# The second layer's quarters 3 and 4: their second product by seven products of halves, and the order of all steps read from a table

## The chip, the cores and the metric

The kernel runs on one core of a Trainium2 chip. The metric is the time of one execution on the device, in microseconds (us). All inputs and outputs are 4-byte floats in the chip's main memory, and the weights arrive as 8-byte words that the kernel itself turns back into 4-byte floats. The engines are named as the profile names them: PE (matmul), PEld (its weight loads, shown apart), DVE (vector), ACT (scalar), POOL, and SP, whose queue issues most of the DMA transfers.

## The reference

A linear attention over 4 x 8 heads of 576 tokens gives 2304 tokens of 512 values each. Two layers of the same shape follow, 512 to 2048 to 512, with a softplus between the two products of the first and an ELU between those of the second:

```python
kv = np.einsum('bhsd,bhse->bhde', k, v)
out = np.einsum('bhsd,bhde->bhse', q, kv)
x = out / np.sqrt(np.mean(out * out, axis=-1, keepdims=True) + 1e-06) * g_norm
h = x @ w_in                       # layer 1: 2304x512 @ 512x2048
g = np.maximum(h, 0.0) + np.log1p(np.exp(-np.abs(h)))
x = g @ w_out                      # 2304x2048 @ 2048x512
h = x @ w_in2                      # layer 2, the same shapes
g = np.where(h > 0.0, h, np.exp(np.minimum(h, 0.0)) - 1.0)
return g @ w_out2
```

## The kernel before

**Precision.** PE works here on 4-byte values that it rounds, so each operand is split into a high and a low part, and a product is three matmuls: high by high, low by high, high by low.

**Tiling.** The 2304 tokens are six blocks of T = 384, taken in three pairs (p). The 2048 inner values are 16 chunks of 128, taken in four quarters (q) of four chunks, each quarter as two pairs of chunks (f). One *slot* is one pair of blocks by one pair of chunks. There are 48 slots: layer 1 has slots 0 to 23, layer 2 slots 24 to 47, with six slots to a quarter, so that layer 2's quarters 3 and 4 are slots 36 to 47. Two slots that follow each other (f = 0, 1) are a *group*; groups 18 to 23 are those two quarters.

**First product.** From slot 4 on it is a seven-product scheme (Strassen's in Winograd's form): the 2 x 2 halves of tokens and of the weights are combined so that seven products of halves, numbered 1 to 7, take the place of eight. `product` (line 788) issues one of them as six matmuls of 384 columns into the PSUM banks A, B or C of the slot. `slot_h` (line 886) ties them together: after product 1, ACT copies A to C (line 928), and product 6 waits for that copy; after products 6 and 7 ACT or DVE copies A to the tiles hj and hk (lines 903, 905), for which products 7 and 4 wait; DVE adds B to hk after product 5 and to hj after product 3 (line 913). Bank B has one buffer: product 5 of the next slot waits for the add to hj, the slot's *closing add*.

**Between.** `elu` (line 996) makes layer 2's activation with ACT and DVE, in a temporary of three buffers (`"e"`). `slot_parts` (line 1222) splits the result for both blocks into G.

**Second product.** In layer 1's quarters 2 to 4 it is by sevens too: `slot_sevens` (line 1050) makes the sums of the halves, and `out_sevens` and `out_piece` (lines 1114, 1121) issue the products in *pieces*. Everywhere else, all of layer 2 included, `slot_out` and `slot_piece` (lines 1234, 1249) multiply plainly: for each block, chunk and third of the tokens three matmuls of 512 columns, 72 to a group; in the last block the last third is cut into two of 256 columns. `block_sum` (line 640) adds the bank to the sums in SBUF, or in the last quarter to an output tile that goes out. `by_sevens` (line 239) says where the sevens are used.

**Weights.** `conv` (line 289) turns a raw chunk into floats (two ACT and three DVE instructions), `split` (line 337) into high and low part, and `split_pair` with `split_sums` (lines 385, 414) makes the sums of halves for the sevens. There is room for about one quarter of weights.

**Order.** All of this is written as strands that run side by side. `Order.run` (line 131) is a planner: it holds costs of each step and keys of urgency, and writes down next whichever step it reckons can start first. PE's steps come from `main` (line 1422), where `STEPS` and `SEVENS` (lines 1309, 1322) say how many pieces stand between the products. The instructions of each engine run in the order in which they were written.

## Time and profile before

| | us |
|---|---|
| median of 3 runs | 804.38 |
| lowest, highest | 804.06, 806.32 |
| the profiled execution | 803.55 |
| its span, first to last instruction | 801.4 |
| PE busy | 788.1 |
| DVE busy | 609.5 |
| ACT busy | 499.2 |
| mean granted clock of PE | 0.998 |

The profiled execution lies 0.83 us under the median, and 2.15 us of it lie outside the span. A matmul's "us" in the timeline includes its way through the array and overlaps its successor; what one costs in a full stream is the distance from its start to the next one's start. The same holds for DVE and ACT, where an instruction's duration is longer than the distance to the next by 0.08 to 0.11 us.

### The profile page before, as it was taken

The numbers are of one execution on the slowest core, as the hardware profiler recorded it, in microseconds if no ns is written. First come the engines' busy times: TensorE is split into PE (matmuls) and PEld (weight loads), VectorE is DVE, ScalarE is ACT, GpSimd is POOL, SyncE is SP. The second block draws the span as 40 slices with busy tenths as digits, with TensorE's granted clock in tenths as the row PEclk, the third lists the DMA queues.
The fourth block names the chain that finished last, engine by engine and source line by source line (L and its number), as shares of the span: only waits on it lengthen the run. The fifth ranks groups of instructions, "written<-read, shape, count | busy, mean of one in ns | idle before, by whom it ended". The sixth has DMA issues, their size and how long they took to land.

```text
span 801.4 us, 12301 instructions
## 1 busy us (share of the span) xinstructions
PE 788.1 (98%) x4586; PEld 744.2 (93%) x4586; DVE 609.5 (76%) x1056; ACT 499.2 (62%) x939; POOL 58.5 (7%) x62
## 2 busy tenths in 40 slices
PE   8999999999999999999997999999999999999998
PEld 7899999999999999999997988988988988989987
DVE  3888887788988889897999976756776768675344
ACT  3886767675675575685677876764754645555331
POOL 3534400000000000000000000000000000000000
PEclk9999999999999999999999999999999999999999
DMA  9999768859668868968284767667567566475512
GB/s 302 335 341 325 274 261 273 295 190 301 234 211 285 263 223 280 294 208 272 77 301 171 270 234 278 245 240 251 185 248 249 170 246 254 151 254 216 182 65 92
DMA packets 46235, 191.25 MB, mean 239 GB/s; under 512 B 5216, under 2 KB 6496, under 8 KB 46176
## 3 DMA queue, kind: packets, MB, share of 16 engines
q1 hardware_dynamic: 44016, 184.57, 64.6%
q0 software_dynamic: 2160, 5.90, 3.9%
q8 instruction: 36, 0.59, 0.3%
q14 instruction: 23, 0.19, 0.1%
HBM read 146.80 MB, written 37.75 MB: 230 GB/s over the span
## 4 chain that ended last, share of the span: by engine, by line
PE 83%; DMA 6%; DVE 5%; ACT 2%; issue 1%; POOL 1%; SPq 0%; DVEq 0%; ACTq 0%
PE A L816 21%; PE B L816 10%; PE acc L1269 10%; PE acc L1270 10%; PE acc L1268 10%; PE A L1152 7%; PE C L816 5%; DMA raw<-w 4%; PE A L844 3%; PE B L1152 3%; PE C L1152 2%; PE po L560 1%; DMA acc_sb<-kv_rest 1%; DMA acc_sb<-kv 1%; PE kv L493 1%
## 5 line engine op out<-in xcount | busy, mean ns | idle before, releaser
L1270 PE MATMUL acc<-wlo,G 128*128 128x512 f32 (+1 forms) x292 | 113.4, 388 | 0.0
L1269 PE MATMUL acc<-whi,G 128*128 128x512 f32 (+1 forms) x292 | 113.3, 388 | 0.0
L1268 PE MATMUL acc<-whi,G 128*128 128x512 f32 (+1 forms) x292 | 112.7, 386 | 0.0
L816 PE MATMUL A<-x,wx 128*128 128x384 f32 x528 | 107.4, 337 | 5.3 <-ACT C L928 3.6
L816 PEld LDWEIGHTS A<-x,wx 128*128 128x128 f32 x528 | 93.3, 189 | 6.8 <-ACT C L928 4.3
L816 PE MATMUL A<-x,whi 128*128 128x384 f32 x352 | 98.6, 335 | 0.6 <-ACT hk L903 0.6
L317 ACT ACTIVATE c<-raw 128x512 f32<-128x512 f32 x64 | 42.9, 671 | 51.7 <-DMA raw<-w 46.1
L816 PEld LDWEIGHTS A<-x,whi 128*128 128x128 f32 x352 | 64.7, 188 | 1.7 <-ACT hk L903 0.9
L1270 PEld LDWEIGHTS acc<-wlo,G 128*128 128x128 f32 x292 | 54.8, 188 | 11.2
L1268 PEld LDWEIGHTS acc<-whi,G 128*128 128x128 f32 x292 | 54.9, 188 | 9.9
L1269 PEld LDWEIGHTS acc<-whi,G 128*128 128x128 f32 x292 | 54.8, 188 | 9.8
L816 PE MATMUL A<-x,wlo 128*128 128x384 f32 x176 | 59.1, 336 | 0.0
L913 DVE TENSOR_TENSOR hj<-hj,B 128x384 f32<-128x384 f32 x44 | 24.3, 552 | 42.9 <-PE B L816 42.7
L347 ACT CAST whi<-q 128x512 fp32r<-128x512 f32 x64 | 39.6, 618 | 24.4 <-PE acc L1269 11.1
L351 DVE TENSOR_TENSOR wlo<-q,whi 128x512 fp32r<-128x512 f32 x64 | 44.0, 687 | 12.9 <-ACT whi L347 12.7
L816 PE MATMUL B<-x,wx 128*128 128x384 f32 x264 | 52.8, 334 | 0.0
L816 PE MATMUL B<-x,whi 128*128 128x384 f32 x176 | 52.1, 336 | 0.0
L816 PE MATMUL C<-x,whi 128*128 128x384 f32 x176 | 52.1, 336 | 0.0
L928 ACT COPY C<-A 128x384 f32<-128x384 f32 x42 | 19.6, 466 | 47.9 <-PE A L816 44.5
L816 PEld LDWEIGHTS B<-x,wx 128*128 128x128 f32 x264 | 46.4, 188 | 0.0
L330 DVE CUSTOM_DVE_ANT_0 q<-c,r 128x1024 uint16<-128x1024 uint16 x64 | 44.0, 687 | 2.1
L325 DVE SCALAR_TENSOR_TENSOR c<-raw,c 128x512 uint32<-128x512 uint32 x64 | 44.0, 688 | 1.0
(231 smaller groups left out, 1901.8 us busy)
## 6 DMA issues: line engine op xcount, KB each, us to landing
x<-spill SPq DMA_DIRECT2D x126, 768.0 KB, 6.2
raw<-w SPq DMA_DIRECT2D x64, 512.0 KB, 5.6
spill<-x SPq DMA_DIRECT2D x42, 768.0 KB, 4.9
acc_sb<-kv SPq DMA_DIRECT2D x16, 512.0 KB, 6.4
acc_sb<-s POOLq DMA_DIRECT2D x15, 384.0 KB, 5.4
out<-o SPq DMA_DIRECT2D x17, 256.0 KB, 2.1
q<-qt SPq DMA_DIRECT2D x9, 256.0 KB, 6.7
q_late<-qt SPq DMA_DIRECT2D x9, 256.0 KB, 6.1
```

What stands on the lines that cost most here:

```text
L317: nc.scalar.activation(c.bitcast(F32), high_f, AF.Copy, scale=2.0**-112)
L325: nc.vector.scalar_tensor_tensor(c, high, 0x80000000, c, op0=ALU.bitwise_and, op1=ALU.bitwise_or)
L330: nc.vector.tensor_tensor(q.bitcast(U32), c, r, op=ALU.add)
L347: nc.scalar.copy(hi, q)
L351: nc.vector.tensor_sub(lo, q, f32(hi))
L816: nc.tensor.matmul(bank[:, :T], w, x, start=start and i == 0, stop=stop and i == len(seq) - 1, skip_group_check=True,)
L844: nc.tensor.matmul(a[:, :T], w, x, start=half == 0 and i == 0, stop=half == 1 and i == len(seq) - 1, skip_group_check=True,)
L913: nc.vector.tensor_add(to, to, bank[:, :T])
L1152: nc.tensor.matmul(a, l, r, start=first and i == 0, stop=last and i == 2, skip_group_check=True)
L1268: nc.tensor.matmul(a, l[0], r[0], start=(u == 0), stop=False)
L1269: nc.tensor.matmul(a, l[1], r[0], start=False, stop=False)
L1270: nc.tensor.matmul(a, l[0], r[1], start=False, stop=(u == QF - 1))
```

## The change

The second product of layer 2's quarters 3 and 4 is computed by seven products of halves, as in layer 1, but with the tokens as rows: the stationary operand is a tile of 128 tokens, the moving one 256 columns of the weights. `by_sevens` returns true there, so the sums of the weights' halves, the sums of the activations' halves and their split follow as in layer 1, behind ELU. `out_piece` issues for each product, slot and part m of the tokens (m = 0 is two tiles of 128, m = 1 the third) six or three matmuls of 256 columns. A new `flush_rows` adds each bank to the SBUF sums with DVE (or, where the result is final, into an output tile, then a DMA of 256 or 128 KB). ELU's temporary is taken from the ring `"s1"`, which has one buffer, in these quarters. The weights' second halves come in as pieces of two chunks.

The planner is gone. `Order.run` reads a table of about 32,000 characters, three to a step (which strand, and which engine or, for PE, whether a product or a piece), so that the order of all engines is fixed there, in both layers. The diff, without the planner's removed lines:

```diff
+    def run(self, table):
+        steps = iter("".join(table.split()))
+        for a, b, letter in zip(steps, steps, steps):
+            s = self.strands[int(a + b, 36)]
+            if s[2] is None:
+                continue
+            self.demand(s[2][1])
             self.now, self.going = s[0], s
             try:
-                s[2] = s[1].send(e)
+                s[2] = s[1].send(self.ENGINES[letter])
             except StopIteration:
-                self.strands.remove(s)
-                continue
-            if e == DMA == s[2][0][0][0]:
-                s[3] = done
+                s[2] = None
...
+TABLE = """
+3pt59p59p59p3pt45t59p59p46t59p59p57t57t47t3qt3pp3pa59p3pa59p3qt3rt59p48p48a59p59p48d3qp59p3rt3st
...
+    SEVENS_FROM = 2
+    OUT_OPS_2 = ((1, 2, 6, 5, 3, 7, 4),) * 3
...
     def by_sevens(layer, q):
-        return layer == 0 and q > 0
+        return q > (0 if layer == 0 else SEVENS_FROM - 1)
...
+        tag = "s1" if a and by_sevens(*slots[s][:2]) else "e"
+        yield ((ACT, act(T if a else 2 * T, True)),), [ring(tag), *ready]
         if not exp_set:
             exp_set.append(s)
             load_set(EXP_SET)
         h = h()[0]
-        e, e_h = sbuf("e", 3, f"e{s}_{b}", (P, 2, T))
+        e, e_h = sbuf(tag, 3 if tag == "e" else 1, f"e{s}_{b}", (P, 2, T))
...
-        bank, a_h = a
-        yield ((ACT, act(T, True)),), [("cc", s)] if b else [("cb", s)]
+        act_of = elu if slots[s][0] else softplus
+        yield from act_of(s, b, h, a, [("cc", s)] if b else [("cb", s)])
         h, h_h = h()
...
+        tiles = range(2 * m, min(2 * m + 2, TT)) if layer else range(1)
+        yield ((PE, 3 * len(tiles) * pe(DM // 2) if layer else 3 * pe(T)),), need
         if f == 0 and o in (1, 5):
             banks[which, m] = psum(("accA", "accT")[o == 5], f"{which}{n}")
-        a = banks[which, m][0][:, :T]
         gh, gl, g_h = g2[s, o]
+        c, n = (0, DM // 2) if layer else (m * P, P)
         if o > 4:
             w = wx_t[layer, fc, 1][0]
-            hi, lo = (w[:, part, o - 5, m * P : m * P + P] for part in range(2))
+            hi, lo = (w[:, part, o - 5, c : c + n] for part in range(2))
         else:
-            c = 256 * (o in (2, 3)) + m * P
-            hi, lo = (w[:, c : c + P] for w in w_t[layer, fc + (o > 2), 1][:2])
+            c += 256 * (o in (2, 3))
+            hi, lo = (w[:, c : c + n] for w in w_t[layer, fc + (o > 2), 1][:2])
         first, last = o in (1, 5) and f == 0, o in (2, 3, 4) and f == FP - 1
-        for i, (l, r) in enumerate(((hi, gh), (lo, gh), (hi, gl))):
-            nc.tensor.matmul(
-                a, l, r, start=first and i == 0, stop=last and i == 2, skip_group_check=True
-            )
+        for k, t in enumerate(tiles):
+            if layer:
+                a = banks[which, m][0][:, k * n : k * n + n]
+                xh, xl = (x[:, t * P : t * P + P] for x in (gh, gl))
+                seq = ((xh, hi), (xh, lo), (xl, hi))
+            else:
+                a = banks[which, m][0][:, :T]
+                seq = ((hi, gh), (lo, gh), (hi, gl))
+            for i, (l, r) in enumerate(seq):
+                nc.tensor.matmul(
+                    a, l, r, start=first and k == i == 0, stop=last and i == 2, skip_group_check=True
...
+        def flush_rows(b, i, name, done, x, x_h):
+
+            rows = acc_sb[2 * p + b].rearrange("p (t n) -> p t n", n=DM)
+            c = slice(DM // 4 * i, DM // 4 * i + DM // 2)
+            to = rows[:, tiles[0] : tiles[-1] + 1, c]
+            x = x.rearrange("p (t n) -> p t n", n=DM // 2)
+            ends = q == NQ - 1 and (o in (2, 3, 4) or o == max(5, 7, key=ops_of(layer, p).index))
+            yield ((DVE, dve(width)),), [ring("q")] if ends else []
+            if ends:
+                r, r_h = sbuf("q", 3, f"o{n_}_{o}")
+                r = r[:, :width].rearrange("p (t n) -> p t n", n=DM // 2)
+                nc.vector.tensor_add(r, to, x)
+            else:
+                nc.vector.tensor_add(to, to, x)
+            if name:
+                mark(name, g, m)
+            if done:
+                drop(x_h)
+            if ends:
+                t0 = (2 * p + b) * T + tiles[0] * P
+                yield ((DMA, dma(P * width * 4)),), []
+                nc.sync.dma_start(
+                    out[t0 : t0 + len(tiles) * P, c].rearrange("(t p) n -> p t n", p=P), r
+                )
+                drop(r_h)
...
+                yield from flush_rows(b, i, name, done, bank[:, :width], bank_h)
+                return
...
-    STEPS = (
-        ((6, '4', 5, 2, '6', '4', 7, 1, 4, '2', 3), (6, '4', 5, 2, '4', 7, '8', 1, 4, 3)),
-        ((6, 2, 5, 7, '5', 1, 4, '1', 3), (6, 2, 5, 7, '1', '16', 4, 1, '1', 3)),
+    PRODUCTS = (
+        ((6, 5, 2, 7, 1, 4, 3), (6, 5, 2, 7, 1, 4, 3)),
+        ((6, 2, 5, 7, 1, 4, 3), (6, 5, 2, 7, 1, 4, 3)),
+        ((6, 2, 5, 7, 1, 4, 3), (6, 2, 5, 7, 4, 1, 3)),
...
+    def main():
+
+        while look("piece") or look(PE):
+            kind = yield ((PE, 0.0),), []
+            step, _, needs = look(kind)
+            order.demand(needs)
+            heads[kind] = None
+            next(step, None)
...
-        order.run()
+        order.run(TABLE)
```

PE's list loses 420 matmuls of 512 columns and 24 of 256, and gains 756 of 256. DVE's list grows from 1056 to 1186 instructions, ACT's from 939 to 984, by the program's own count.

**Place 1, the border of the layers (slots 25 and 26).** ACT's list of before from just behind the copy A25 to hk25 to the copy A26 to C26. G24 and G25 are the split activations of slots 24 and 25, e25 ELU's temporary, c and r steps of `conv`, s11 copies of banks for layer 1's sums, x1 operands of layer 2.

```order
L1227 CAST G24_1_4861<-hk24_4645 128x768
L347 CAST whi1_0_1_4871<-q1_0_1_4802 128x512
L1227 CAST G24_0_4881<-hj24_4559 128x768
L317 ACTIVATE c1_1_1_4884<-raw1_1_1_4852 128x512
L1006 ACTIVATE e25_1_4895<-A25_4667 128x384
L320 ACTIVATE r1_1_1_4898<-raw1_1_1_4852 128x512
L1009 ACTIVATE e25_1_4895<-hk25_4859 128x384
L1180 COPY s11_0_3_4902<-B11_0_4727 128x384
L1011 ACTIVATE e25_1_4895<-e25_1_4895 128x768
L1180 COPY s11_0_3_4902<-B11_1_4738 128x384
L747 CAST x1_0_1_2_4910<-acc_sb2_71 128x768
L928 COPY C26_4913<-A26_4874 128x384
```

The same stretch of ACT's list after the change, with the copy to hk25 itself at its head:

```order
L957 COPY hk25_4859<-A25_4667 128x384
L1321 CAST G24_1_4861<-hk24_4645 128x768
L374 ACTIVATE c1_1_1_4863<-raw1_1_1_4850 128x512
L377 ACTIVATE r1_1_1_4885<-raw1_1_1_4850 128x512
L1274 COPY s128_3_4896<-B11_0_4727 128x384
L1321 CAST G24_0_4898<-hj24_4601 128x768
L1274 COPY s128_3_4896<-B11_1_4734 128x384
L982 COPY C26_4901<-A26_4872 128x384
```

Between the two copies 11 instructions stood; now 6 do. ELU's three steps of slot 25 and two operand casts stand behind the copy to C26.

PE's list there, before: the end of product 3 of slot 25 (bank B25), product 6 of slot 26 (bank A26) and what follows.

```order
L816 MATMUL B25_4835<-x1_0_0_3_4620,wlo1_3_0_4782 128x384
L816 MATMUL B25_4835<-x1_0_0_3_4620,whi1_3_0_4772 128x384 x2
L816 MATMUL A26_4874<-x1_0_1_6_4832,wx1_0_0_4324 128x384 x6
L816 MATMUL C26_4913<-x1_0_1_2_4910,whi1_0_0_4173 128x384
L816 MATMUL C26_4913<-x1_0_1_2_4910,wlo1_0_0_4179 128x384
```

After:

```order
L874 MATMUL B25_4835<-x1_0_0_3_4547,wlo1_3_0_4783 128x384
L874 MATMUL B25_4835<-x1_0_0_3_4547,whi1_3_0_4780 128x384 x2
L1362 MATMUL acc1_0_0_1_0_4916<-whi1_0_1_4852,G24_1_4861 128x512
L1363 MATMUL acc1_0_0_1_0_4916<-whi1_0_1_4852,G24_1_4861 128x512
L1364 MATMUL acc1_0_0_1_0_4916<-wlo1_0_1_4879,G24_1_4861 128x512
L1362 MATMUL acc1_0_0_1_1_4920<-whi1_0_1_4852,G24_1_4861 128x512
L1363 MATMUL acc1_0_0_1_1_4920<-whi1_0_1_4852,G24_1_4861 128x512
L1364 MATMUL acc1_0_0_1_1_4920<-wlo1_0_1_4879,G24_1_4861 128x512
L1362 MATMUL acc1_0_0_1_2_4924<-whi1_0_1_4852,G24_1_4861 128x512
L1363 MATMUL acc1_0_0_1_2_4924<-whi1_0_1_4852,G24_1_4861 128x512
L1364 MATMUL acc1_0_0_1_2_4924<-wlo1_0_1_4879,G24_1_4861 128x512
L874 MATMUL A26_4872<-x1_0_1_6_4831,wx1_0_0_4321 128x384 x6
```

Three pieces (nine matmuls of 512 columns) of slot 24's second product stand between slot 25's product 3 and slot 26's product 6, where there was nothing.

**Place 2, quarter 3 to 4 (slots 41 and 42).** DVE's list of before, from the closing add of slot 41 to the add of B42 to hk42:

```order
L913 TENSOR_TENSOR hj41_7101<-hj41_7101,B41_7109 128x384
L1026 SCALAR_TENSOR_TENSOR hk41_7142<-e41_1_7247,hk41_7142 128x384
L351 TENSOR_TENSOR wlo1_15_0_7285<-q1_15_0_7082,whi1_15_0_7274 128x512
L1229 TENSOR_TENSOR G41_1_7291<-hk41_7142,G41_1_7291 128x768
L1026 SCALAR_TENSOR_TENSOR hj41_7101<-e41_0_7139,hj41_7101 128x384
L905 COPY hk42_7321<-A42_7238 128x384
L1016 SCALAR_TENSOR_TENSOR hj42_7289<-e42_0_7302,C42_7255 128x384
L913 TENSOR_TENSOR hk42_7321<-hk42_7321,B42_7293 128x384
```

After, the first 12 of the 23 rows of the same stretch (acc_sb are the sums in SBUF, A19 and B19 banks of group 19's pieces, xk and xj split sums of halves):

```order
L967 TENSOR_TENSOR hj41_7230<-hj41_7230,B41_7244 128x384
L1125 TENSOR_TENSOR hk40_7127<-hj40_7080,hk40_7127 128x384
L1249 TENSOR_TENSOR acc_sb2_71<-acc_sb2_71,B19_0_7308 128x2x256
L1127 TENSOR_TENSOR hj40_7080<-hk40_7127,hj40_7080 128x384
L1249 TENSOR_TENSOR acc_sb3_72<-acc_sb3_72,A19_0_7152 128x2x256
L1130 TENSOR_TENSOR hj40_7080<-hj40_7080 128x384
L1249 TENSOR_TENSOR acc_sb3_72<-acc_sb3_72,A19_1_7165 128x256
L1071 SCALAR_TENSOR_TENSOR hj41_7230<-e41_0_7368,C41_7186 128x384
L483 TENSOR_TENSOR wx1_14_0_7298<-t2_1_14_0_7300,wx1_14_0_7298 128x256
L1159 TENSOR_TENSOR xk1_40_7428<-hk40_7127,xk0_40_7427 128x768
L1159 TENSOR_TENSOR xj1_40_7431<-hj40_7080,xj0_40_7430 128x768
L1081 SCALAR_TENSOR_TENSOR hj41_7230<-e41_0_7368,hj41_7230 128x384
```

Where 8 instructions stood, 23 stand.

**Place 3, the end (slot 47 and group 23).** DVE's list of before from slot 47's closing add on (o are output tiles):

```order
L913 TENSOR_TENSOR hj47_7920<-hj47_7920,B47_7924 128x384
L1016 SCALAR_TENSOR_TENSOR hk47_7950<-e47_1_8029,A47_7877 128x384
L1026 SCALAR_TENSOR_TENSOR hk47_7950<-e47_1_8029,hk47_7950 128x384
L1026 SCALAR_TENSOR_TENSOR hj47_7920<-e47_0_7934,hj47_7920 128x384
L1229 TENSOR_TENSOR G47_1_8062<-hk47_7950,G47_1_8062 128x768
L1229 TENSOR_TENSOR G47_0_1_8069<-hj47_7920,G47_0_0_8068 128x768
L665 TENSOR_TENSOR o5_0_0_8091<-acc_sb5_74,acc1_3_2_1_0_8041 128x512
L665 TENSOR_TENSOR o5_1_0_8096<-acc_sb5_74,acc1_3_2_1_1_8047 128x512
```

After, a stretch behind the same add (x12, x4, xj, xk are group 23's operands by halves):

```order
L1159 TENSOR_TENSOR xk1_46_8498<-hk46_8260,xk0_46_8497 128x768
L1247 TENSOR_TENSOR o22_0_4_8517<-acc_sb3_72,A22_0_8245 128x512
L1119 TENSOR_TENSOR x12_47_8502<-hj47_8347,x12_47_8502 128x768
L1071 SCALAR_TENSOR_TENSOR hk47_8396<-e47_1_8500,A47_8232 128x384
L1081 SCALAR_TENSOR_TENSOR hk47_8396<-e47_1_8500,hk47_8396 128x384
L1247 TENSOR_TENSOR o22_1_4_8533<-acc_sb3_72,A22_1_8278 128x256
L1141 TENSOR_TENSOR x4_47_8548<-hk47_8396,x4_47_8548 128x384
L1145 TENSOR_TENSOR hk47_8396<-hk47_8396 128x384
L1125 TENSOR_TENSOR hk47_8396<-hj47_8347,hk47_8396 128x384
L1127 TENSOR_TENSOR hj47_8347<-hk47_8396,hj47_8347 128x384
L1130 TENSOR_TENSOR hj47_8347<-hj47_8347 128x384
L1159 TENSOR_TENSOR xj1_46_8487<-hj46_8215,xj0_46_8486 128x768
```

and ACT's list after the change at the same place (C23 are copies of group 23's banks):

```order
L1061 ACTIVATE e47_1_8500<-A47_8232 128x384
L1117 CAST x12_47_8502<-hj47_8347 128x768
L1064 ACTIVATE e47_1_8500<-hk47_8396 128x384
L1066 ACTIVATE e47_1_8500<-e47_1_8500 128x768
L1139 CAST x4_47_8548<-hk47_8396 128x384
L1233 COPY C23_0_8550<-A23_0_8524 128x512
L1233 COPY C23_1_8556<-A23_1_8544 128x256
L1157 CAST xj_47_8587<-hj47_8347 128x768
L1157 CAST xk0_47_8589<-hk47_8396 128x768
```

The operands of the last pieces now take a longer way over both engines, and C23's copies stand behind x4_47.

## Rows read from the trace of the kernel before

**Rows 1.** The page: busy us, share, instructions by engine; the chain by engine.

```profile
PE 788.1 (98%) x4586; PEld 744.2 (93%) x4586; DVE 609.5 (76%) x1056; ACT 499.2 (62%) x939; POOL 58.5 (7%) x62
...
PE 83%; DMA 6%; DVE 5%; ACT 2%; issue 1%; POOL 1%; SPq 0%; DVEq 0%; ACTq 0%
```

**Rows 2.** Waits of PE: engine, line, releaser; us in total, times, longest.

```profile
PE A L816 <- ACT C L928: 3.6, 2, 3.5
...
PE A L816 <- ACT hj L903: 1.4, 1, 1.4
```

**Rows 3.** Timeline of PE near the end: start us, us, what, count.

```profile
782.30 0.39 PE L1268 MATMUL acc<-whi,G 128*128 128x512 f32 x1
...
795.25 0.28 PE L1268 MATMUL acc<-whi,G 128*128 128x256 f32 x1
...
798.00 0.28 PE L1270 MATMUL acc<-wlo,G 128*128 128x256 f32 x1
...
797.52 0.19 PEld L1270 LDWEIGHTS acc<-wlo,G 128*128 128x128 f32 x1
```

**Rows 4.** Timeline of PE at the layers' border.

```profile
429.75 1.20 PE L816 MATMUL A<-x,wx 128*128 128x384 f32 x6
...
434.40 0.51 PE L816 MATMUL B<-x,whi 128*128 128x384 f32 x2
438.40 2.29 PE L816 MATMUL A<-x,wx 128*128 128x384 f32 x6 [3.49 <-ACT C L928]
...
441.70 0.51 PE L816 MATMUL C<-x,whi 128*128 128x384 f32 x2
```

**Rows 5.** Timeline of ACT at the layers' border.

```profile
430.99 0.48 ACT L903 COPY hk<-A 128x384 f32<-128x384 f32 x1
431.36 0.84 ACT L1227 CAST G<-hk 128x768 fp32r<-128x768 f32 x1
432.10 0.62 ACT L347 CAST whi<-q 128x512 fp32r<-128x512 f32 x1
...
433.75 0.67 ACT L317 ACTIVATE c<-raw 128x512 f32<-128x512 f32 x1 [0.29 <-DMA raw<-w]
434.32 0.47 ACT L1006 ACTIVATE e<-A 128x384 f32<-128x384 f32 x1
...
435.66 0.47 ACT L1180 COPY s<-B 128x384 f32<-128x384 f32 x1
436.02 0.85 ACT L1011 ACTIVATE e<-e 128x768 f32<-128x768 f32 x1
...
437.86 0.49 ACT L928 COPY C<-A 128x384 f32<-128x384 f32 x1
```

**Rows 6.** Windows: stretch, its us, then busy us of each engine, granted clock.

```profile
300.00:390.00 90.00, 90.00 (x521) 90.00 (x520) 79.05 (x148) 58.80 (x115) 4.42 (x5) 1.00 0.75 247
392.00:430.00 38.00, 37.56 (x213) 36.35 (x212) 37.15 (x64) 26.08 (x47) 1.75 (x2) 1.00 0.57 194
438.40:441.80 3.40, 3.40 (x11) 3.40 (x12) 2.86 (x4) 2.71 (x5) 0.11 (x1) 0.53 0.91 215
593.00:697.00 104.00, 104.00 (x525) 94.17 (x524) 74.47 (x129) 59.69 (x111) 0.00 (x0) 1.00 0.62 220
697.00:801.00 104.00, 101.28 (x508) 90.55 (x506) 51.69 (x84) 39.88 (x74) 0.00 (x0) 1.00 0.46 162
```

**Rows 7.** Timeline of DVE in the second layer, instructions back to back.

```profile
663.10 0.42 DVE L403 TENSOR_TENSOR t<-q,q 128x256 f32<-128x256 f32 x1
663.43 0.55 DVE L913 TENSOR_TENSOR hk<-hk,B 128x384 f32<-128x384 f32 x1
663.90 0.42 DVE L405 TENSOR_TENSOR t<-q 128x256 f32<-128x256 f32 x1
664.24 0.95 DVE L1229 TENSOR_TENSOR G<-hj,G 128x768 fp32r<-128x768 f32 x1
665.11 0.42 DVE L407 TENSOR_TENSOR t<-q,t 128x256 f32<-128x256 f32 x1
```

More of the change, by code (lines that the diff above doesn't have):

```diff
@@ L168, in run, with demand @@
+        return i < 0 or all(h[0] <= 0 for h in held[: i + 1][-n:])
+    def demand(self, needs):
+        for need in needs:
+            if not self.met(need):
+                raise RuntimeError(f"not there yet: {need}")
+    def run(self, table):
[5 more added lines that the diff above has]
+            self.demand(s[2][1])
             self.now, self.going = s[0], s
@@ L1124, in out_piece @@
         fc = q * QF + 2 * f
[L1125 removed]
+        ends = [max(x, key=ops_of(layer, p).index) for x in ((1, 2), (3, 4), (5, 6, 7))]
         which = {1: "A", 6: "A", 7: "A", 4: "A", 2: "C", 5: "B", 3: "B"}[o]
@@ L1356, in one @@
-    def one(pieces):
-        if pieces:
-            yield pieces.head[1], [pieces.ready]
-            pieces.take()
-    def some_of(pieces, n):
-        for _ in range(n):
-            yield from one(pieces)
-    def filler():
-        for s in range(FP, FILLED):
-            while s in pieces_of and pieces_of[s]:
-                yield from one(pieces_of[s])
-    pieces_of = {}
-    def ready(need):
-        at = [order.when(n) for n in need]
-        return None if None in at else max(at, default=0.0)
@@ new lines, in all_pieces, with look @@
+            for b in (0, 1) if g < PLAIN else (1, 0):
+                yield from slot_out(layer, q, p, b, g == LAYERS * SLOTS // FP - 1 and b == 0)
+    work = {PE: all_products(), "piece": all_pieces()}
+    heads = {}
+    def look(kind):
+        if not heads.get(kind):
+            work_ = next(work[kind], None)
+            heads[kind] = work_ and (work_, *next(work_))
+        return heads[kind]
+    def main():
[5 more added lines that the diff above has]
+            next(step, None)
@@ L1500, in linear_attention_then_two_ffns @@
         make_identity(nc, ident)
-        order.free.update({DMA: 800.0, ACT: 1900.0, DVE: 3300.0, PE: 1300.0})
         mark("ident")
```

366 lines of the change are left out of this document (162 added, 204 removed).

## The prediction

> **What bounds the kernel now.** I read the page first. PE is busy 98% of the span, the chain that ended last runs through PE for 83% of it, and DVE and ACT are busy 76% and 62% [rows 1]. So I looked for what PE loses, in its waits: after the first 100 us, which the change touches little, there are two that matter, 3.5 us for ACT's copy to C at the border of the layers and 1.4 us for a copy to hj [rows 2]. Elsewhere PE streams; the first 104 us of quarters 3 and 4 have no gap at all [rows 6]. There a matmul costs its distance to the next one: 0.227 us for 512 columns (57 of them from 782.30 to 795.25), 0.120 for 256 (23 steps from 795.25 to 798.00, or 0.1196) [rows 3], 0.173 for 384 (six in 1.20 us, of which the last way through the array is 0.34) [rows 4]. So the time is PE's list at these distances, and the change has two questions: how much shorter the list gets, and whether DVE and ACT, which must do more, can still feed it.
>
> All sums below go against the profiled execution, 803.55 us, of which 801.4 are the span; the median lies 0.83 above it.
>
> **1. PE's list.** Removed: 420 x 0.2272 = 95.4 us and 24 x 0.1196 = 2.9. Added: 756 matmuls of 256 columns, at 0.120 each 90.7. Together **-7.6 us**. By the 0.1196 of the row it is -7.9. That row is from a tail in which the other engines have little to do, so as the other end I allow 2% more for a matmul, 0.122, which gives -6.1. Each matmul also needs a weight load, and there are 312 more of them. The load of a 256-column piece takes 0.19 us, longer than the 0.120 of its step, and the stream keeps its step all the same [rows 3], so I add nothing.
>
> **2. The border.** Product 6 of slot 26 could have started at 434.40 + 2 x 0.173 = 434.75 and started at 438.40, behind the copy to C26: 3.65 us [rows 4]. ACT was the reason [rows 5]: it began the copy hk25 at 430.99 and ended C26's at 437.86 + 0.49 = 438.35, with eleven instructions in between. Then the granted clock of the next 3.4 us is 0.53 [rows 6], the lower level of 1.2 GHz for most of it, after PE had stood for 3.65 us: the ten matmuls from 438.40 to 441.70 take 3.30 us in place of 10 x 0.173 = 1.73 [rows 4], another 1.57. The stall costs 5.2 us.
>
> After the change six instructions stand between the two copies. By the distances there (copy 0.37, G 0.74, c 0.57 and r as much, s 0.36, G 0.74, s 0.36, copy 0.49) the copy to C26 ends 4.2 us after hk25's began. PE meanwhile has three products, 18 x 0.173 = 3.1, and now three pieces, 9 x 0.227 = 2.0: 5.1 us. The wait is covered with 0.9 to spare, and with PE running on, as from 300 to 390 [rows 6], I take the clock at its upper level. What was queued behind comes later: ELU of slot 25, two casts, and DVE's adds that read them. Next late is DVE, which from the closing add of slot 24 to the add to hk26 has 49 instructions, 28.6 us at the distances below, against PE's 28.0. I take **-4.6 us** (0.6 for DVE), with ends -5.2 and 0. Before that, the same chain was longer on ACT than on PE by the 3.65 that the rows show.
>
> **3. DVE through slots 37 to 45.** In place of adds of 512 columns DVE gets sums of halves, their low parts, weight sums and more adds of banks. By size: 54 more instructions of 256 columns, 60 of 384, 5 of 512, 12 of 768. From start to start these take 0.335, 0.47 and 0.87 us [rows 7], and 512 lies between, 0.60. That is 18.1 + 28.1 + 3.0 + 10.4 = 59.7 us more work on DVE, nearly all of it in the 208 us of these quarters, where it was busy 74.5 + 51.7 = 126 [rows 6]. ACT gets some 22 us more onto 59.7 + 39.9 [rows 6]: it has room.
>
> Over the whole it fits: 186 of 200 us. Where it is tight I counted between the closing adds of slots 37 and 45. There DVE has 226 instructions (57 of 256, 87 of 384, 59 of 512, 23 of 768), 115.5 us; PE has 27 x 0.227 + 336 x 0.173 + 450 x 0.120 = 118.1. So DVE must be busy 98% of the time for PE to run on (before: 75 of 123.5 us). The tightest place inside is slot 41's closing add to the add to hk44: 81 instructions, 41.7 us, against PE's 42.7. At the change of quarter alone, where 23 instructions stand for 8, it is 12.0 against 12.7. The margin is some 1 us in each, and behind a late closing add stands product 5 of the next slot on PE, since B has one buffer.
>
> Can DVE run at 98% of a stretch? In 392 to 430 it was busy 37.15 of 38 us, and PE 37.56 of 38: that cost PE 0.44 us [rows 6]. From 300 to 390 it was at 88%, and PE lost nothing [rows 6]. The first is the nearest row; scaled from 38 to 118 us it gives 0.44 x 3.1 = 1.4. I take **+1.5 us**, with ends 0 and +6 (rival B carries the far end).
>
> The Trainium skill, "Perfetto Trace Analysis", section "Tensor Engine Instruction (MATMUL, LD_WEIGHTS)", says that ACT, DVE and GpSimd each run their instructions strictly first in, first out. The trace agrees where ACT's copy C26 stood behind work that nobody waited for. By that rule one late instruction on DVE delays all that I counted, and the sum would lean to rival B.
>
> **4. The tail.** Before, the last group's adds and casts are few, and its 512-column pieces run to the end with no gap [rows 3]. After, the operands of group 23 go through both engines. Behind slot 47's last product PE has 48 matmuls of other groups, 5.75 us, until the first piece that reads x12_47. DVE's list to there is about 5.5 us, but in it stands o22_0_4, which needs the bank of group 22's product 4: about 6.1, a stall of 0.3. Then C23_0's copy stands behind x4_47 on ACT, some 0.8; xj1_46 needs 4.5 us more of DVE against 30 matmuls, 3.6: up to 0.9 of which I take half; and products 2, 3 and 4 each hand a bank to DVE or ACT and get it back, 0.15 to 0.3 each. Sum **+2.0 us** (1 to 3). The last transfer has the same size as before, 128 x 256 values, so nothing is added behind it.
>
> **5. The rest: 0, within 1.5 either way.** The bytes are the same; SP issues 8 more transfers of raw weights (shorter ones) and 5 more outputs, each 7 to 13 apart over 200 us, with DMA busy 46 to 62% [rows 6]. ELU's temporary in one buffer costs nothing while DVE reads it in time (rival C). The order of the first layer, now from the table, differs from the planner's in few places; the 1.4 us at hj [rows 2] wait for a late transfer and I leave them in.
>
> **Sum:** -7.6 - 4.6 + 1.5 + 2.0 = **-8.7 us**: a span of 792.7, a profiled execution of 794.85, and with the 0.83 a median of **795.7 us**.
>
> **The rivals.**
>
> *B, DVE becomes the bound in slots 37 to 45.* For it: 98% needed, one-buffered bank B behind it, and each DVE instruction that waits for PE or ACT (sums of halves need both ELU halves) is a hole that cannot be made good. Against it: 392 to 430 [rows 6]. If DVE can use 92% of the stretch, midway between the 88% and the 98% of the two stretches in [rows 6], rounded down, 115.5 us of work take 125.5, that is 7.4 over PE's 118.1 in place of 1.5: 801.6 us. Chance 0.17.
>
> *C, ELU's temporary holds ACT, and the kernel is slower.* "s1" has one buffer, so ACT's first ELU step of the second block stands until DVE has read the first block's, and behind it in ACT's list stand the copies hk and C that products 4 and 6 wait for (before, "e" had three buffers). With DVE at 98% that read can be late. A stall as long as the border's costs 5.2 us with the slow clock behind it. The gain without it is 8.7, so the kernel becomes slower by more than 2.4 us only from three such stalls on (11.1 / 5.2 = 2.1); four give 795.7 + 20.8 = 816.5. Against it: DVE's reads stand early in its list, and ACT is busy under 60% [rows 6]. Chance 0.05.
>
> *D, the border's stall stays,* since the pieces put there wait for their own operands (G24's low part or wlo1_0_1 on DVE) just when PE should have had them as cover: the 4.6, and 0.6 of the slow clock more, are not won: 800.9. Against it: the first of these is ACT's first instruction behind hk25. Chance 0.10.
>
> *E, a 256-column matmul isn't half a 512-column one (slower too).* Against it: 0.120 against 0.227 [rows 3]. If the 0.19 us of its weight load were its step once the other engines are busy, PE's list would grow by 756 x 0.19 - 98.3 = 45 us and the time would be some 849. Chance 0.02.
>
> The Trainium skill, "TensorE: Matmul & The Clock Gate", section "Back-to-back issue gap", gives a sustained distance of about 81 ns at 128 columns and 131 ns at 512, which interpolates to 98 ns at 256. By that estimate the change to PE's list would be 756 x 0.098 - 420 x 0.131 - 24 x 0.098 = +16.7 us and the time about 820. The rows differ: 227 and 120 ns for these operands, so the distance nearly follows the columns, and the row decides.
>
> **How the numbers follow.** Forecast 0.62; B 0.17; D 0.10; C 0.05; E 0.02; better than forecast, with DVE and tail at no cost and the first layer's order gaining something, 0.04 (about 790). The likeliest is 795.7. The forecast alone, with the bounds of terms 1, 3 and 4, runs from 792 to 800. The range reaches down to 790.5 for term 5 and up to 802.5, so that it takes in B and D; what is left out is C, E, the far end of B and something below. A measurement of this kernel can tell about 0.3% from no change, 2.4 us: faster is below 802.0, slower above 806.8. The forecast, the better case and about 0.17 of B and D together are faster: 0.83. The rest of B and D is the same: 0.10. C and E are slower: 0.07.
>
> **What would show it.** PE's busy time falls by 6 to 8 us (1). At the border no wait for the copy to C26 of over 0.6 us, and a granted clock of 1.0 there (2); a wait of 3 us or more there is D. From slot 37 to 45 DVE is busy 95% or more, and PE's waits there add up to under 3 us (3); if PE's waits for DVE's adds to hj and hk add up to 6 us or more, B is right; if they are for ACT's copies while ACT itself waits for DVE, C. In the last 15 us PE has gaps of 1 to 3 us, behind x12_47, C23 and xj1_46 (4). The prediction is wrong if the span falls by more than 12 us, or if distances between 256-column matmuls in the stretch exceed 0.125.

## The result, and the profile after

The changed kernel takes 793.65 us (median of 4 runs, 792.27 to 794.88) against 804.22 for the kernel before on the same chip: a ratio of 0.9865, with a 95% interval of 0.9841 to 0.9888. A second series on another chip gave 795.52 against 804.39, 0.9891 (0.9878 to 0.9905). The forecast was 795.7 within 790.5 to 802.5. The profiled execution took 794.88 us, its span is 793.1; it is the slowest of the four, with a mean granted clock of 0.994 where the other three have 0.999 to 1.0.

The page after, busy time by engine and the chain that ended last by engine, to be read beside [rows 1]:

```profile
PE 781.8 (99%) x4898; PEld 754.8 (95%) x4898; DVE 663.4 (84%) x1186; ACT 520.8 (66%) x984; POOL 59.2 (7%) x62
...
PE 92%; DVE 4%; DMA 1%; ACT 1%; issue 1%; SPq 0%; DVEq 0%; ACTq 0%
```

PE is still the bound, and more so: 92% of the chain in place of 83%. All of PE's waits of 0.5 us and more in the profile after (us in total, times, longest), beside [rows 2]:

```profile
PE po(0, 0)_168 L617 <- DMA q<-qt: 2.1, 1, 2.1
PE warm L1476 <- DVE kvf L1490: 1.4, 1, 1.4
PE A L874 <- ACT hk L957: 1.1, 1, 1.1
PE A L1216 <- DVE o L1247: 0.7, 2, 0.5
PE A L1216 <- DVE xj L1159: 0.7, 1, 0.7
PE A L1476 <- ACT hj L936: 0.6, 1, 0.6
```

The wait for the copy to C26 and the one at 289 us are gone. New are 2.1 us at the start, for the first q, 0.6 at 42 us, and three short waits at the end; the wait for the copy to hk25, just ahead of the border, has grown from 0.6 to 1.1 us. Between 600 and 770 us, where DVE got its new work, PE waits for nothing.

Three windows of the profile after (stretch, its us, busy us of PE, PEld, DVE, ACT, POOL with their instructions, granted clock, busy share of the DMA engines, GB/s): slots 37 to 45 between their closing adds, the pieces at the border, and the last stretch:

```profile
616.60:735.30 118.70, 118.64 (x815) 117.24 (x814) 116.52 (x227) 83.78 (x158) 0.00 (x0) 1.00 0.65 235
...
434.60:436.70 2.10, 2.10 (x11) 1.71 (x11) 2.10 (x4) 2.10 (x5) 0.87 (x1) 1.00 0.18 49
...
770.00:788.85 18.85, 17.30 (x132) 15.87 (x130) 13.70 (x25) 4.48 (x8) 0.00 (x0) 1.00 0.27 91
```

The first row is the sharpest test of the prediction: DVE is busy 116.52 of 118.70 us, 98.2%, and PE 118.64.

To see where the time went I sum for each matmul its distance to the next one's start less the usual distance of its width (0.2272, 0.1733, 0.1196 us for 512, 384, 256 columns, 0.110 and 0.029 for the 128 and 64 of the attention). What is left over is PE's loss, by stretch; with PE's list (the count of its matmuls at these distances) and the time before the first and behind the last matmul's start it adds up to the span. A wait costs PE more here than its row says: its idle time counts from the end of the matmul before it, which overlaps what follows in a full stream, and the second matmul behind it is late too. For the copy to hk25 that is 1.38 us for a wait of 1.11, for xj1_46's first 0.95 for 0.69, so about 0.27 each. All in us, worked out from the traces of this study; below I call this table the ledger:

| kernel | list | 0 to 100 | to 425 | to 445 | to 590 | to 760 | to last | behind | span |
|---|---|---|---|---|---|---|---|---|---|
| before | 773.7 | 10.6 | 3.0 | 6.6 | 1.3 | 1.2 | 0.1 | 3.4 | 801.4 |
| changed | 765.8 | 13.3 | 0.1 | 1.9 | 1.9 | 0.7 | 3.5 | 4.5 | 793.1 |
| plain_neworder | 773.7 | 11.4 | 0.4 | 2.1 | 1.2 | 1.4 | 0.1 | 3.4 | 795.2 |
| sevens_oldorder | 765.8 | 10.0 | 3.6 | 6.8 | 1.4 | 0.8 | 3.5 | 4.5 | 797.9 |
| dve12 | 765.8 | 12.0 | 0.8 | 2.1 | 1.7 | 3.1 | 3.5 | 4.5 | 795.0 |
| dve48 | 765.8 | 14.1 | 0.1 | 1.8 | 1.9 | 18.1 | 3.8 | 4.5 | 811.6 |
| border_pe | 765.8 | 10.8 | 1.0 | 2.9 | 1.7 | 0.7 | 3.5 | 4.6 | 792.5 |
| border_act | 765.8 | 12.9 | 0.1 | 2.6 | 1.9 | 0.7 | 3.5 | 4.5 | 793.5 |
| border_both | 765.8 | 12.8 | 0.6 | 6.1 | 1.7 | 0.8 | 3.5 | 4.5 | 797.3 |
| gn_late | 765.8 | 14.3 | 1.1 | 1.8 | 2.0 | 0.7 | 3.5 | 4.6 | 795.2 |
| after_again | 765.8 | 14.1 | 0.1 | 1.9 | 1.9 | 0.7 | 3.5 | 4.5 | 793.9 |
| head_old | 765.8 | 10.2 | 1.5 | 2.2 | 1.6 | 0.7 | 3.5 | 4.5 | 791.5 |
| best2 | 765.8 | 10.7 | 1.2 | 2.7 | 1.6 | 0.7 | 3.7 | 4.0 | 791.9 |

(The time before the first matmul, 1.4, is left out of the columns. The stretches are of time, so what stands at their edges differs a little between kernels.)

From before to changed: list -7.9, start +2.7, to 425 -2.9, border -4.7, then +0.6 and -0.5, end +3.4 and +1.1: -8.3 before rounding.

### The profile page after: what moved, and what is told of

It is laid out like the page before. It is cut to its first block, busy times and chain, and to the rows that moved or that the text cites. A ratio compares the mean times of both kernels' runs of the same rounds, so it can differ in the third digit from the quotient of the medians.

```text
span 793.1 us, 13152 instructions
## 1 busy us (share of the span) xinstructions
PE 781.8 (99%) x4898; PEld 754.8 (95%) x4898; DVE 663.4 (84%) x1186; ACT 520.8 (66%) x984; POOL 59.2 (7%) x62
## 4 chain that ended last, share of the span: by engine, by line
PE 92%; DVE 4%; DMA 1%; ACT 1%; issue 1%; SPq 0%; DVEq 0%; ACTq 0%
PE A L874 23%; PE A L1216 13%; PE B L874 11%; PE B L1216 7%; PE acc L1363 6%; PE acc L1364 6%; PE acc L1362 6%; PE C L874 6%; PE A L902 4%; PE C L1216 3%; PE kv L550 1%; PE po L617 1%; PE warm L1476 1%; PE pt L689 1%; DMA q<-qt 1%
## 5 line engine op out<-in xcount | busy, mean ns | idle before, releaser
L874 PE MATMUL A<-x,whi 128*128 128x384 f32 x352 | 100.8, 335 | 1.1 <-ACT hk L957 1.1
L1364 PE MATMUL acc<-wlo,G 128*128 128x512 f32 x144 | 56.7, 394 | 0.0
L1363 PE MATMUL acc<-whi,G 128*128 128x512 f32 x144 | 56.6, 393 | 0.0
L1362 PE MATMUL acc<-whi,G 128*128 128x512 f32 x144 | 56.0, 389 | 0.0
L377 ACT ACTIVATE r<-raw 128x512 uint32<-128x512 uint32 x64 | 42.8, 669 | 2.6 <-DVE wx L483 2.6
L1216 PE MATMUL A<-x,whi 128*128 128x384 f32 x144 | 41.2, 334 | 0.0
L957 ACT COPY hk<-A 128x384 f32<-128x384 f32 x36 | 17.3, 481 | 36.3 <-PE A L874 32.3
L834 DVE TENSOR_TENSOR x<-acc_sb,x 128x768 fp32r<-128x768 f32 x38 | 35.6, 950 | 3.3 <-ACT x L804 3.2
L1289 POOL DMA_DIRECT2D acc_sb<-s x15 | 13.4, 892 | 321.8 <-ACT s L1274 219.7
```

The lines of the kernel that those rows point to most:

```text
L377: nc.scalar.activation(r, low, AF.Copy, scale=2.0**-29)
L834: nc.vector.tensor_sub(t[:, 2:, :], x, f32(t)[:, :2, :])
L874: nc.tensor.matmul(bank[:, :T], w, x, start=start and i == 0, stop=stop and i == len(seq) - 1, skip_group_check=True,)
L1216: nc.tensor.matmul(a, l, r, start=first and k == i == 0, stop=last and i == 2, skip_group_check=True)
L1362: nc.tensor.matmul(a, l[0], r[0], start=(u == 0), stop=False)
L1363: nc.tensor.matmul(a, l[1], r[0], start=False, stop=False)
```

## The experiments

The order of all engines is a table in the changed kernel. The old order can be written as such a table too, and the two can be joined at the start of a slot, since the arithmetic is the same in both up to the second layer's quarter 3. That gives the two halves of the change: the order up to slot 31, and the sevens together with the order that they need behind it.

**plain_neworder: the order up to slot 31 alone.** The new table up to slot 31's first product, the old order from there, and plain products everywhere:

```
-    SEVENS_FROM = 2
+    SEVENS_FROM = 4
```

> The change's order of all engines up to the start of slot 31 (past the border of the layers), then the old order, with the old plain second product everywhere. Theory (the gain has two halves, about 4 us from the order and 4 us from the arithmetic): the border's stall is gone (-4.7 us by the two profiles), the waits between 100 and 425 us are gone (-3.0), the first 100 us are 2.7 us longer, 0.6 is lost again behind the border: about 4.4 us under the kernel before, 799 to 801 us, and its last 350 us take as long as before. Rival 1 (the gain is the arithmetic's alone, the order earns nothing): 803.5 to 805. Rival 2 (the longer first 100 us in the profile after belong to that one execution and not to the order): about 7 us under before, 796.5 to 798.

797.51 us against 802.96, a ratio of 0.9932 (0.9917 to 0.9947), 5.5 us less. That lies between the theory (4.4 less) and rival 2 (7 less), nearer the theory; the time itself falls into rival 2's range, but the kernel before was faster on this chip, by 1.3 us. Rival 1 is out. In the ledger the border loses 2.1 in place of 6.6, the stretch ahead of it 0.4 in place of 3.0, and the start 11.4: less than the 13.3 of the changed kernel's profile by the same order. So part of that 13.3 belongs to the execution, as rival 2 has it.

**sevens_oldorder: the sevens alone.** The old order up to slot 31, the changed table from there, the sevens in quarters 3 and 4.

> The old order of all engines up to the start of slot 31, so that the border's stall of 3.65 us and the slow clock behind it are there again, then the change's order and its sevens in quarters 3 and 4. Theory: PE's list is shorter by 7.9 us, DVE costs nothing in slots 37 to 45, the tail costs 4.2 us: 3.5 to 4.5 us under the kernel before, 799.5 to 801 us; PE waits 3 to 4 us for the copy to C26. Rival (DVE, at 98% in slots 37 to 45, needs the table's order from the start to come to that stretch without arrears): PE's waits for DVE there add up to 3 us or more, 803 us or more.

800.05 us, 0.9958 (0.9943 to 0.9974): 3.4 us less by the ratio and 2.9 by the medians, just under the theory's 3.5 to 4.5 and far from the rival. The border's stall is back (PE's longest wait in this profile):

```profile
PE A L874 <- ACT C L982: 3.5, 1, 3.5
```

The rival falls: the stretch from 590 to 760 us loses 0.8 us, as little as with the new table. The product of the two ratios is 0.989, beside 0.9865 and 0.9891 for the whole change: the two halves add up to it.

**dve12 and dve48: is DVE at its edge?** PE waits for nothing while DVE is busy 98.2%. Either it stands just short of being the bound, or its work has more room than its busy time says. So I add work that nobody reads:

```
+    junk = const.tile([P, T], F32, name="junk")
...
+            if 18 <= g <= 21 and m == 0 and o in (2, 5, 3):
+                nc.vector.tensor_add(junk, junk, junk)
```

In dve48 the condition is only `18 <= g <= 21`.

> The changed kernel with 12 more adds of 384 columns on DVE, three in each of groups 18 to 21, right behind the adds of banks; nobody reads what they write. That is 12 x 0.47 = 5.6 us more work between slots 37 and 45, where DVE was busy 116.5 of 118.7 us. Theory (DVE has about 2 us left there and no more): 3 to 4 us longer, in PE's waits for DVE's adds to hj and hk. Rival (DVE's work can lag: what is late in slots 37 to 45 is made good behind them, and PE does not wait at the closing adds): under 1 us longer.

> The changed kernel with 48 more adds of 384 columns on DVE, one behind every add of a bank in groups 18 to 21: 48 x 0.47 = 22.6 us more work between slots 37 and 45. Theory (about 2 us left, everything above lengthens the kernel one to one): 19 to 21 us longer. Rival (work can lag to slots 45 to 47, where DVE has 5 of 30 us free): 13 to 16 us longer; if DVE had much more room than counted, under 10.

796.78 and 813.4 us, single runs. By the ledger the stretch from 590 to 760 us loses 3.1 and 18.1 in place of 0.7: 2.4 us of 5.6 added, and 17.4 of 22.6 (and 0.3 more behind 760). Both lie between the theory (3 to 4, 19 to 21) and its rival (under 1, 13 to 16), the first nearer the theory, the second about halfway. Some 3 to 5 us of added work find room and not 2; of the 16.9 us between the two runs 15 lengthen the stretch. The lower end of the room is what the count leaves: 118.7 us less 115.5 of DVE's work from start to start are 3.2; the busy time leaves 2.2, since it counts each instruction's end that overlaps the next. The waits are not where I put them. PE's waits between 600 and 770 us, first of dve12, then of dve48 (cut):

```profile
PE A L1217 <- DVE acc_sb L1250: 1.6, 2, 1.4
```

```profile
PE A L1217 <- DVE acc_sb L1250: 5.0, 3, 2.4
PE A L1217 <- DVE o L1248: 1.6, 1, 1.6
...
PE A L875 <- DVE hk L1072: 1.3, 3, 0.5
PE B L875 <- DVE hk L968: 0.9, 1, 0.9
```

L1250 is the add of a bank of the sevens to the sums in SBUF. The pieces are what waits first, for their banks A, and not product 5 for the closing add. But the added adds stand right behind the adds of banks; whether work added elsewhere would make the closing adds wait first was not tried. And DVE runs on at its limit (the stretch of slots 37 to 45 by its old times, in dve12):

```profile
616.60:735.30 118.70, 117.04 (x802) 114.97 (x801) 117.91 (x233) 82.81 (x157) 0.00 (x0) 1.00 0.63 226
```

99.3% busy, and PE has lost only 1.7 us there.

**border_pe, border_act, border_both: which cover ends the stall?** The change puts two things at the border, three pieces of PE ahead of product 6 and a shorter row of ACT ahead of the copy to C26. Each is put back alone, then both (ACT's list in border_act and border_both; in border_pe the nine matmuls go behind product 7):

```
 L1274 COPY s_3<-B_1 128x384
+L1061 ACTIVATE e_1<-A 128x384
+L1064 ACTIVATE e_1<-hk 128x384
+L1066 ACTIVATE e_1<-e_1 128x768
+L804 CAST x_0_1_2<-acc_sb 128x768
 L982 COPY C<-A 128x384
```

> The changed kernel, with the three pieces that stand between slot 25's product 3 and slot 26's product 6 put back behind slot 26's product 7; ACT's order stays the changed one. In the profile after, PE ended product 3 at about 434.6 and the copy to C26 ended at 435.02. Theory (ACT's order ends most of the stall, the pieces a rest): product 6 waits 0.5 us, up to 1.1 by the working in the prediction, the granted clock stays 1.0, the kernel is longer by no more than 1.5 us. Rival (the pieces are the cover): a wait of about 3.5 us and a low clock behind it, 5 us longer.

> The changed kernel, with four of ACT's instructions (three of ELU of slot 25 and one operand cast) put back between the copies to hk25 and C26; the three pieces stay where the change has them. Theory: the copy to C26 ends 2.4 us later, at 437.4, against PE's cover to 436.7: product 6 waits 0.6 to 0.9 us, the clock stays 1.0. Rival (ACT's order is what counts): a wait of over 2 us.

> The changed kernel with both put back, the pieces behind product 7 and the four instructions of ACT ahead of the copy to C26. Theory: the two covers add up: the wait is 2.4 + 0.5 = 2.9 us, and a slow clock behind it costs up to 1.6 more, so that the stretch from 425 to 445 us loses 3 to 4.5 us more than in the changed kernel. Rival (the stall has another cause, as the bank or the operands of slot 26): 1 us or less.

Product 6 of slot 26 on PE's timeline, in border_pe, border_act and border_both (start, us, what, count, idle time before it and releaser):

```profile
433.61 1.31 PE L874 MATMUL A<-x,wx 128*128 128x384 f32 x6 [0.32 <-ACT C L982]
```

```profile
437.19 1.34 PE L874 MATMUL A<-x,wx 128*128 128x384 f32 x6 [0.62 <-ACT C L982]
```

```profile
437.58 1.57 PE L874 MATMUL A<-x,wx 128*128 128x384 f32 x6 [2.72 <-ACT C L982]
```

Either cover alone does nearly all: the border's stretch loses 1.0 and 0.7 us more than in the changed kernel. Without both it loses 4.2 more: 2.7 us of waiting, and a lower clock behind it. The window behind that wait in border_both:

```profile
436.50:441.00 4.50, 3.42 (x13) 3.42 (x14) 3.88 (x6) 4.50 (x9) 0.00 (x0) 0.72 0.86 192
```

The granted clock is 0.72 there, part of the stretch at the lower level of 1.2 GHz. The same window of the changed kernel, where PE runs on:

```profile
436.50:441.00 4.50, 4.50 (x27) 4.46 (x26) 4.50 (x6) 4.50 (x10) 0.00 (x0) 1.00 0.93 194
```

The theory held in all three, and both rivals of a single cause fell.

**gn_late: the start.** The 2.1 us wait for q at 7 us is new, and in SP's list two small transfers of g_norm now stand ahead of the third transfer to q. They go back:

```
-L582 DMA q_139<-qt 128x512 x2
-L1483 DMA gn<-g_norm 64x1 x2
-L582 DMA q_139<-qt 128x512
+L582 DMA q_139<-qt 128x512 x3
...
+L1483 DMA gn<-g_norm 64x1 x2
 L361 DMA raw_1_0_239<-w 128x512
```

> The changed kernel with one step of its table moved: the two small transfers of g_norm, which stand in SP's queue ahead of the third transfer to the first q, go behind raw_0_0 and the next q, as in the kernel before. Nothing else moves. Theory (PE's 2.1 us wait for q at 7 us, and the lower clock behind it, come from this place in the queue, since all four profiles with the new order have that wait at 1.8 to 2.2 us and the two with the old order 0.3 or none): the wait falls to 0.5 us or less and the kernel is 2 to 3 us shorter, 790.5 to 792. Rival (the wait is the memory's, or the rest of the head's order takes the gain back before 100 us): within 1 us of the changed kernel, 793 to 794.5.

796.85 us, 0.9895 (0.9873 to 0.9917): no gain. The wait for q is gone, and others have come; PE's timeline of the first 100 us in gn_late, the rows with idle time before them, but for the wait of 1.4 us at the very start, which is in all kernels (the last row's 0.58 is in the kernel after too, the first two are new):

```profile
9.48 0.80 PE L550 MATMUL kv<-acc_sb 128*64 128x64 f32 x20 [1.24 <-DMA acc_sb<-kv]
23.15 1.16 PE L617 MATMUL po(1, 0)_315<-kvf,q 128*64 128x128 f32 x4 [2.29 <-ACT kvf L564]
43.70 0.71 PE L1476 MATMUL A<-ident 128*128 128x128 f32 x4 [0.58 <-ACT hj L936]
```

The start loses 14.3 us, more than the changed kernel's 13.3. My theory of one cause fell. ACT's timeline shows where the longer of the new waits comes from:

```profile
19.38 0.58 ACT L652 ACTIVATE acc_sb<-po(0, 0)_166,gn 128x384 f32<-128x384 f32 x1 [4.17 <-DMA gn<-g_norm]
```

ACT stood 4.17 us for g_norm itself, the transfer that was moved back, and the copies to kvf that PE waits for stand behind that instruction in ACT's list. In the kernel after, with g_norm early, ACT has no wait for it. So the new order of ACT needs g_norm early, and its old place in the queue was no improvement.

**head_old and best2, with the changed kernel again beside them.** If no single step makes the start longer, its whole order may. head_old takes the old order up to slot 8's first product, about 105 us, and the changed table from there. best2 adds three small things: four output tiles, an add moved on DVE and a copy moved on ACT:

```
-                r, r_h = sbuf("q", 3, f"o{n_}_{o}")
+                r, r_h = sbuf("q", 4, f"o{n_}_{o}")
```

```
 L1119 TENSOR_TENSOR x_47<-hj,x_47 128x768
+L1247 TENSOR_TENSOR o_1_4<-acc_sb,A 128x256
 L1071 SCALAR_TENSOR_TENSOR hk<-e_1,A 128x384
 L1081 SCALAR_TENSOR_TENSOR hk<-e_1,hk 128x384
-L1247 TENSOR_TENSOR o_1_4<-acc_sb,A 128x256
```

```
+L957 COPY hk<-A 128x384
 L804 CAST x_0_1_5<-s_1_1 128x768
 L1069 ACTIVATE e_0<-e_0 128x384
-L957 COPY hk<-A 128x384
```

> The changed kernel unchanged, beside the next two on one chip, to compare them with it. 0.984 to 0.989 of the kernel before.

> The changed kernel with the old order of all engines up to the start of slot 8 (about 105 us), the changed order from there. In eight profiles the first 100 us lost 10.0 and 10.6 us on PE with the old order, 10.8 to 14.3 with the new one (mean 12.5). Theory (the new order of the head costs about 2 us, which my prediction put at nothing): 1.5 to 2.5 us under the changed kernel on the same chip, and the first 100 us lose 10 to 10.6 us. Rival (the head is bound by its transfers and differs by execution, not by order; whatever is won is waited for again before 100 us): within 1 us of the changed kernel.

> As head_old, and besides: the ring of output tiles has four buffers in place of three; on DVE the add to o22_1_4 stands ahead of the two ELU steps of hk47; on ACT the copy to hk25 stands ahead of an operand cast and an ELU step. Theory: the wait of 0.7 us for o22_1_4 goes (0.3 to 0.6), the last adds no longer wait for an output tile (0.4 to 0.7), the wait for hk25 falls from 1.1 to 0.3 us (0.8): 1.5 to 2 us less than head_old. Rival (the tail's chain through x4_47 and xj1_46 is only made later by the moved add, and what is won at hk25 is waited for at the copy to C26): within 0.5 us of head_old.

head_old takes 792.32 us, 0.985 (0.9836 to 0.9864), against 795.52 and 0.9891 (0.9878 to 0.9905) for the changed kernel on the same chip: 3.2 us less, and the intervals don't meet. The start loses 10.2 us in place of 14.1; 1.4 come back as waits between 100 and 425. So the order of the start cost the change some 2.5 us by the profiles and 3.2 by the medians on this chip, and head_old is the fastest kernel there; the changed kernel's first series, 0.9865 (0.9841 to 0.9888) on another chip, overlaps it. The windows of the first 30 us, head_old and then the kernel after:

```profile
0.00:10.00 10.00, 8.46 (x73) 7.74 (x73) 2.61 (x7) 2.19 (x4) 1.01 (x9) 1.00 0.72 254
10.00:30.00 20.00, 19.28 (x235) 16.78 (x234) 12.51 (x23) 13.95 (x35) 11.13 (x12) 1.00 1.03 357
```

```profile
0.00:10.00 10.00, 6.47 (x47) 5.99 (x48) 2.06 (x6) 1.70 (x3) 0.73 (x7) 0.96 0.71 214
10.00:30.00 20.00, 19.97 (x220) 17.75 (x219) 10.26 (x19) 11.98 (x29) 9.21 (x10) 0.85 0.99 326
```

Behind the wait of 2.1 us the granted clock is 0.85 for the next 20 us; in head_old, where PE has no such wait, it is 1.00. Most of the price goes with that clock: the two profiles with the new order in which it stayed at 1.00 lose 10.8 and 11.4 us at the start (border_pe, plain_neworder), hardly more than the four with the old order (10.0 to 10.7).

best2 takes 793.36 us, 0.9866 (0.985 to 0.9882), no better than head_old: 0.4 us longer by the profiles, as the rival has it, and 1.0 by the medians, with intervals that meet. Each thing did its own part, and two gave it away at the next wait. The wait for o22_1_4 has become one for the copy C23, and hk25's is shorter by 0.5 us, with a new one for a low part of weights right behind it. From best2's waits of PE:

```profile
PE C L1216 <- ACT C L1233: 0.8, 1, 0.8
...
PE A L874 <- ACT hk L957: 0.6, 1, 0.6
...
PE acc L1364 <- DVE wlo L408: 0.5, 1, 0.5
```

Only the fourth output tile was won, by the trace; the time doesn't tell it from nothing. The last two adds on DVE, in the kernel after and in best2:

```profile
788.71 1.02 DVE L1247 TENSOR_TENSOR o<-acc_sb,A 128x512 f32<-128x512 f32 x2 [1.77 <-DMA out<-o]
```

```profile
787.56 1.14 DVE L1247 TENSOR_TENSOR o<-acc_sb,A 128x512 f32<-128x512 f32 x2 [1.33 <-PE A L1216]
```

With three tiles the first of them waits for an earlier output to leave; with four it waits for PE, and the time behind the last matmul falls from 4.5 to 4.0 us.

## Why the prediction was right, point by point

**1. PE's list: right.** -7.6 was forecast; at the 0.1196 of the row the list is shorter by 7.9 us. In the busy stretch the price holds, with DVE at 98% beside it: the mean distance of 452 matmuls of 256 columns is 0.1202 us there, by which it would be 7.4 (what a matmul takes above 0.1196 stands in the table's columns). PE's timeline of the kernel after, first from that stretch, then from the end, where DVE has little to do:

```profile
647.86 2.32 PE L1216 MATMUL A<-wx,xk 128*128 128x256 f32 x18
...
779.41 2.32 PE L1216 MATMUL B<-wx,xk 128*128 128x256 f32 x18
```

Eighteen in 2.32 us, of which the last way through the array is 0.28: (2.32 - 0.28) / 17 = 0.120. The 2% that I allowed for company were not needed, and the 312 further weight loads stayed hidden; rival E is out.

The estimate of 98 ns, interpolated between two figures of the Trainium skill ("TensorE: Matmul & The Clock Gate", section "Back-to-back issue gap"), is not what these operands take here, in either stretch: 120 ns.

**2. The border: right.** -4.6 forecast, -4.7 measured, by the mechanism named: the stall's 5.2 us are gone. The 0.6 set against it for a late DVE came only in part: 0.2 us at 441.7, where PE met a late step of ELU on DVE. Another 0.5 was lost to ACT's copy to hk25, and a loss of before, 0.55 us for a sum of weights on DVE at 426 us, went. That these three nearly cancel, and the term comes out within 0.1, is luck. The working put ACT's list at 4.2 us from hk25's copy to the end of C26's; in the profile after it was 434.51 + 0.51 - 430.83 = 4.19 (ACT's timeline):

```profile
430.83 0.47 ACT L957 COPY hk<-A 128x384 f32<-128x384 f32 x1
...
434.51 0.51 ACT L982 COPY C<-A 128x384 f32<-128x384 f32 x1
```

What the working didn't say is that the two covers are nearly interchangeable: either alone leaves only 0.3 or 0.6 us of the wait for C26's copy.

The Trainium skill ("Perfetto Trace Analysis", section "Tensor Engine Instruction (MATMUL, LD_WEIGHTS)") has ACT as strictly first in, first out, and border_act agrees: four instructions whose results product 6 doesn't read, put ahead of the copy that it waits for, make PE wait 0.62 us.

**3. DVE in slots 37 to 45: the load right, its price too high.** 226 instructions and 98% were forecast, and 116.52 of 118.70 us came. The term of +1.5 measured -0.5 (0.7 us lost from 590 to 760, 1.2 before). The step that failed is the scaling of 392 to 430 [rows 6], where PE lost 0.44 us in 38: those 0.44 us are two waits for DVE, 0.27 for a sum of weights and 0.17 for an add of a bank, that belong to their place in the old order and not to DVE's share. PE's waits in the kernel before from 392 to 430 us:

```profile
PE A L816 <- DVE wx L426: 0.3, 1, 0.3
PE A L1152 <- DVE acc_sb L1183: 0.2, 1, 0.2
```

In the new order DVE is nearly as full there, 97.2%, and PE has no gap (window of the kernel after):

```profile
390.00:428.00 38.00, 38.00 (x221) 38.00 (x220) 36.95 (x65) 27.10 (x48) 1.75 (x2) 1.00 0.59 195
```

DVE at 98.2% costs nothing in slots 37 to 45, and rival B lies 3 to 5 us of DVE's work away, by dve12 and dve48. The claim that a late closing add is what PE would meet first did not come true there either.

**4. The tail: too low by 2.5.** +2.0 forecast (1 to 3; its items as listed add up to 2.0 to 2.45), 4.5 measured: 3.4 on PE and 1.1 behind its last matmul. Of the waits named, the 0.8 for C23's copy did not come, and xj1_46's came whole. In place of C23's there are two for banks of group 22 that DVE had not yet emptied. PE's timeline after:

```profile
770.82 0.38 PE L1216 MATMUL A<-whi,x 128*128 128x256 f32 x1 [0.19 <-DVE o L1247]
...
773.03 0.38 PE L1216 MATMUL A<-whi,x 128*128 128x256 f32 x1 [0.53 <-DVE o L1247]
...
777.13 2.45 PE L1216 MATMUL A<-wx,xj 128*128 128x256 f32 x16 [0.69 <-DVE xj L1159]
```

By the distances, with the late matmul behind each, the first two cost 0.45 and 0.79 us, xj1_46 and the operand behind it 1.2, where I had taken 0.45, and three hand-overs of banks 0.3 each, the upper end of my 0.15 to 0.3 (the first matmul behind one takes 0.38 us in place of 0.28). And "nothing is added behind the last transfer" was wrong: the last adds waited for an output tile (0.5 us by best2), and the last transfer, of the same size, took 2.1 us from issue to landing in place of 1.7. The one ahead of it is twice as large as before and was issued 0.5 us earlier in place of 1.4; whether that is why was not tried.

**5. The rest: 0 forecast, and two terms that cancel.** The order of the first layer is not different "in few places" only: DVE's and ACT's lists part at their 12th and 13th instruction. It was worth -2.9 us between 100 and 425 us and about +2.7 in the first 100. I had put the 1.4 us at 289 us down as staying, and the start at nothing, having read SP's list only in the second layer's quarters. That the sum came out at 0.4 with the later 0.6 was luck within the 1.5 allowed.

**The rivals.** D, a stall that stays, did not come. C, the one-buffered temporary: ACT does stand, for the temporary (second row) and far longer for work of DVE that it reads (first row), and PE doesn't notice. Two of ACT's waits between 600 and 770 us in the kernel after:

```profile
ACT e L1077 <- DVE hj L967: 17.4, 8, 7.2
...
ACT e L1061 <- DVE hk L1081: 3.1, 4, 1.5
```

Up to 7.2 us at a time, and no wait of PE follows; ACT had that much time.

So the forecast of 795.7 lies 0.2 to 2 us from the two medians with errors of -0.3, -0.1, -2.0, +2.5 and +0.4 in its five terms. That sum is 0.5, because the third and the fourth cancel: the two terms that were sized wrong differ in sign, and that is luck, not method. For the profiled execution the working gave 794.85, and 794.88 was measured (1.8 us of it outside the span, in place of 2.15); the other three executions of that series lie 1.1 to 2.6 us lower.
